# Output weights split in the first pass of the gated stage; eight scalings issued one at a time; last row tiles in order 0, 2, 1, 3

## Chip, cores and metric

The kernel runs on one core of a Trainium2 chip. The metric is the device time of one execution in microseconds (us). TensorE is called PE (its weight loads PEld), VectorE DVE, ScalarE ACT, GpSimd POOL; SP is SyncE, whose queue issues every DMA of this kernel.

## What is computed

Local-window and global attention over 4 batches give x of 2304 tokens by 512. Two feed-forward stages follow:

```
h = x @ w_in                      # 512 -> 2048
x = elu(h) @ w_out                # 2048 -> 512
rms = sqrt(mean(x*x, -1) + 1e-6)
xn = x / rms * rms_g
out = (silu(xn @ w_gate) * (xn @ w_val)) @ w_o2     # 512 -> 1536 -> 512
```

All is float32. The products run in PE's fp32r format: every operand is divided into a high part (an ACT cast) and the rest (a DVE subtraction), and three products of the parts (`PASSES`) are summed. Such a division is called a split below.

## The kernel before

**First stage.** `moe_block(b, slot)` works on 512 tokens, b from 0 to 3, in 16 slots j. A slot runs a first product `mm1` (12 matmuls into `h`), and a second product `mm2` of the slot before (12 matmuls into `y`); the attention of the next block lies between. Block 3 carries, in slots 0 to 9, the global attention (`g_S`, `g_T`, `g_PV`, `g_X`), and in slots 10 to 15 the 128 global rows' own first stage (`second_mm1`, `second_mm2`) and the preparation of the gated stage (`second_slot`: norms of y, splits of the operands).

**Output weights.** The gated stage multiplies 2x2 blocks by a Strassen-like scheme of seven products. The seven sums of blocks of `w_o2` are made in blocks 1 to 2 and written to DRAM as `wF`: 21 units of 128 x 512 floats (256 KB), two to a group, 11 groups. Before the change block 3 turns them into split form: in the last part of slots 0 to 8 and in the first two parts of slot 9, `h_split(n)` casts each unit of a group into a tile of the pool `stg` (two buffers), subtracts in place, and stores both parts to `wH` (42 stores of 256 KB); then `h_load` fetches the group after next into a pool of two buffers (`hp`). The gated stage reads `wH` back (`w_load`) when it needs it.

**Start of the gated stage.** At the end of slot 9 `second_start()` closes the pools of the global attention and issues the loads of the matrix of ones, of the first 1024 tokens of y (`ya`, `yb`, 1 MB each) and of the first three groups of input weights (`fetch`, 512 KB each into one of three `wraw` buffers). `y_square` (four ACT squares and three POOL sums), `y_root` (one PE product `ms`, a square root and a DVE reciprocal) and `y_norm` (four DVE scalings of 128 x 512) follow for each half.

**Gated stage.** `for k in range(2)` takes 1024 tokens at a time: six iterations i of 14 products (`product`, six matmuls of 512 columns each) with ACT copies (`take`), DVE sums (`add_to`), `gate` and `times`, into `p`; then seven passes n that multiply `p` by `wH`. The input weights come in 42 groups, 21 for each k: `need(q)` splits groups (an ACT cast and a DVE subtraction of 128 x 1024) one or two ahead of the product that uses them, and each split fetches a further group. Tiles of these splits, of `p` and of the operands `xc` share the 16 slots of the pool `wpool`. While k = 0 runs, the second 1024 tokens are prepared: `y_square(1, .)` at the ends of i = 1 and 2, `y_root(1, .)` within i = 2 and 3, `y_norm(1, 0)` and `y_norm(1, 1)` at the ends of i = 2 and 3, `y_sums(1)` at the end of i = 4.

**Last pass.** With k = 1 and n = 6, four row tiles t of 128 tokens are finished one after the other. `ch[0]` holds t = 0, 1 and `ch[1]` holds t = 2, 3. After each, half a bank is copied to an `o4` tile of `stg` and stored. The rows of the global tokens (`og`) leave through `stg` just before.

**Order.** PE runs its instructions in the order in which they are written. For the other engines and the DMA queue the framework orders the instructions at build time by a planner with its own cost estimates; `behind(mark)` tells it to place what is inside after the last pair of instructions noted in `mark`. Each engine then runs its list in order, so that an instruction which waits holds all behind it, and SP holds all DMAs behind one that waits.

Of the kernel before, what the change touches and what calls it, by code (L numbers as in the profile page):

```python
# [7 lines left out]
F32 = mybir.dt.float32  # L8
F32R = mybir.dt.float32r
# [4 lines left out]
ALU = mybir.AluOpType  # L14
# [19 lines left out]
def f(ap):  # L34
    return ap.bitcast(F32)
# [7 lines left out]
def fused_kernel(ctx: ExitStack, tc: tile.TileContext, kq, vl, gkq, gv, w_in, w_out, w_gate, w_val, w_o2, rms_g, consts, out):  # L43
# [102 lines left out]
    @contextmanager  # L146
    def behind(pair):
        with tc.issue_after(pair[0].ins), tc.issue_after(pair[1].ins):
            yield
# [447 lines left out]
        fetch()  # L597

    wraws, n_fetch, groups = [], [0], {}
    n_split, wmark = [0], []  # L600

    def fetch():
        while len(wraws) < 3 and n_fetch[0] < 42:
            raw = bpools["raw"].tile([P, 1024], F32, tag="wraw", name="wraw")
            parts, q, end = raw.rearrange("p (s a n) -> p s a n", s=4, a=2), 4 * (n_fetch[0] % 21), 4 * (n_fetch[0] % 21) + 4
            while q < end:
                i, r = divmod(q, 14)
                m = min(14 - r, end - q)
                nc.sync.dma_start(out=parts[:, 4 - (end - q):4 - (end - q) + m],
                                  in_=wS[i // 2, :, r:r + m, :, P * (i % 2):P * (i % 2) + P])  # L610
                q += m
            wraws.append(raw)
            n_fetch[0] += 1

    def split(n=1):
        for _ in range(n):
            if n_split[0] >= 42:
                return
            raw = wraws.pop(0).rearrange("p (a n) -> p a n", a=8)
            t = wpool.tile([P, 8, 2, P], F32R, tag="w", name="wS")  # L620
            groups[n_split[0]] = t
            n_split[0] += 1
            hi = nc.scalar.copy(t[:, :, 0, :], raw)  # L623
            wmark[:] = hi, nc.vector.tensor_tensor(out=t[:, :, 1, :], in0=raw, in1=f(t[:, :, 0, :]), op=ALU.subtract)  # L624
            fetch()

    def need(q):
        while q not in groups:
            with behind(mark):
                split()  # L630
# [30 lines left out]
            nc.vector.reciprocal(rs, rs)  # L661
            rs_[k, h] = rs

    def y_norm(k, h):
        if k < 2:
            y = ys_[k][h]
            for c in range(4):
                nc.vector.scalar_tensor_tensor(out=y[:, c], in0=y[:, c], scalar=gcol[:, c:c + 1], in1=rs_[k, h], op0=ALU.mult, op1=ALU.mult)

    def y_sums(k):  # L670
        if k < 2:
# [105 lines left out]
    def product(ps, k, i, pos, m, first=True):  # L777
        q, base = 14 * i + 2 * pos + m, 21 * k
        need(base + min(20, q // 4 + (q % 4 > 0) + 1))
        w, x = groups[base + q // 4], X[XSETS[pos]]  # L780
        for c in range(2):
            for z, (ws, xs) in enumerate(PASSES):
                nc.tensor.matmul(ps, w[:, 2 * (q % 4) + c, ws, :], x[:, c, xs, :], start=(first and c == 0 and z == 0), stop=(c == 1 and z == 2),  # L783
                                 skip_group_check=True)
# [86 lines left out]
    xd = xgp.tile([P, 2, 2, P], F32R, name="xd")  # L871
    with ExitStack() as gs:
        gp = gs.enter_context(tc.tile_pool(name="gp", bufs=1))
        hp = gs.enter_context(tc.tile_pool(name="hp", bufs=2))
        zero = gp.tile([P, 64], F32, name="zero")[:, 0:1]
        nc.vector.memset(zero, 0.0)
        G = {}
# [71 lines left out]
            nc.tensor.transpose(x[:64, :], d["e"], ident)  # L949
            nc.scalar.copy(xg32[64 * par:64 * par + 64, :, b * 32:b * 32 + 32], x[:64, :].rearrange("d (a q) -> d a q", a=4))  # L950

        wf_t = []

        def h_load():
            n = len(wf_t)
            if n < 11:
                t = hp.tile([P, 2, 2, 256], F32, tag="wf", name="wf")
                nc.sync.dma_start(out=t if n < 10 else t[:, :1], in_=wF[n] if n < 10 else wF[n, :, :1])
                wf_t.append(t)

        def h_split(n):
            for q in range(2 if n < 10 else 1):
                t = wf_t[n][:, q]
                hi = stg.tile([P, 2, 256], F32, tag="stg", name="wh")
                nc.scalar.copy(hi.bitcast(F32R), t)
                nc.vector.tensor_tensor(out=t.bitcast(F32R), in0=t, in1=hi, op=ALU.subtract)
                for z, part in enumerate((hi, t)):
                    nc.sync.dma_start(out=wH[n, :, q, z], in_=part)
            h_load()

        def slot3(j, part, h):
            g = act1(h, 512) if part == 0 else None
            b = j // 2
            if j < 8:
                if j % 2 == 0:
                    if part < 2:
                        g_S(b, part)
                    elif b:
                        g_PV(2 * b - 1)
                        g_load_v(2 * b + 1)  # L980
                        g_X(2 * b - 2)
                elif part < 2:
                    g_T(2 * b + part)
                else:
                    g_load_k(b + 1)
                    g_PV(2 * b)
                    g_load_v(2 * b + 2)
                    if b:
                        g_X(2 * b - 1)
            elif j == 8 and part == 2:  # L990
                g_PV(7)
                g_X(6)
            elif j == 9 and part == 0:
                g_X(7)
                xg32 = G["x"]
                nc.scalar.copy(xg[:, :, 0, :], xg32[:, :, :P])
                nc.vector.tensor_tensor(out=xg[:, :, 1, :], in0=xg32[:, :, :P], in1=f(xg[:, :, 0, :]), op=ALU.subtract)
            if j < 9 and part == 2 or j == 9 and part < 2:
                with behind(mark):
                    h_split(j + part * (j == 9))  # L1000
            if j == 9 and part == 2:
                gs.close()
                second_start()
            if j >= 10:
                if part == 0:
                    if 0 <= j - 11 < 4:
                        gg[j - 11] = g_act(gg.pop("e"))
                    if j - 12 < 3:
                        second_mm2(j - 12)
                    second_mm1(j - 10)  # L1010
                if part == 2:
                    second_slot(j - 10)
            return g
# [1 line left out]
        g_load_k(0)  # L1015
        g_load_v(0)
        g_load_v(1)
        h_load()
        h_load()
        moe_block(3, slot3)  # L1020
        second_mm2(3)
        ysb = moe.tile([P, 2, 512], F32, tag="xT3", name="ysb")
# [8 lines left out]
    for k in range(2):  # L1031
        pp = []
        for i in range(6):
# [15 lines left out]
            for z in range(2):  # L1049
                product(Q[z], k, i, 1, z)  # L1050
                add_to(t1[:, z], Q[z])
                if z == 0:
                    gate(t1[:, 0])
            times(p[:, 0], t1[:, 0], t1[:, 1])
            if k:
                if i == 0:
                    with behind(mark):
                        x_split(1, ("B22",))
                tile_products(i, 1)
            for z in range(2):  # L1060
                product(A[z], k, i, 2, z, False)
                take(t2[:, z], A[z])
                if z == 0:
                    if k == 0 and i == 1:
                        g_root(*yg)
                    elif i in (2, 3):
                        y_root(k + 1, i - 2)
            Q = [aps.tile([P, 512], F32, tag="att", name="Q") for _ in range(2)]
            for z in range(2):
                product(Q[z], k, i, 3, z)  # L1070
# [2 lines left out]
            for z in range(2):  # L1073
# [3 lines left out]
                if z == 0:  # L1077
                    gate(t3[:, 0])
            times(p[:, 3], t3[:, 0], t3[:, 1])
            for z in range(2):  # L1080
                product(A[z], k, i, 5, z, False)
            if k:
# [1 line left out]
            e = moe.tile([P, 512], F32, tag="e", name="s", bufs=2)  # L1084
            mark[0] = nc.scalar.activation(e, A[0], AF.Silu)
            times(p[:, 1], e, A[1])
            if i == 5:
                h_n, h_p, w_t = [0], [], []
                w_load(w_t)
                w_load(w_t)  # L1090
                for _ in range(3):
                    prepare(h_n, h_p, pp, k)
# [5 lines left out]
            times(p[:, 2], t2[:, 0], t2[:, 1])  # L1098
            nc.vector.tensor_tensor(out=p[:, 2], in0=p[:, 2], in1=p[:, 3], op=ALU.add)
            if k == 0:  # L1100
                if i == 0:
                    y_load(1)
                elif i == 1:
                    y_square(1, 0)
                elif i == 2:
                    y_square(1, 1)
                    y_norm(1, 0)
                elif i == 3:
                    y_norm(1, 1)
                elif i == 4:  # L1110
                    y_sums(1)

# [8 lines left out]
        for n in range(7):  # L1121
# [8 lines left out]
                    prepare(h_n, h_p, pp, k)  # L1130
            order_ = [(i, t) for i in range(6) for t in range(4)]
            if k and n == 6:
                order_ = [(i, t) for t in range(4) for i in range(6)]
            for i, t in order_:
                q = 6 * n + i
                while len(w_t) < min(11, q // 4 + 3):
# [18 lines left out]
                    elif n == 5:  # L1155
                        tile_out(i, 1, 1, w, False, i == 5)
                if k and n == 6 and i == 5:
                    if t % 2 == 0:
                        o4 = stg.tile([P, 512], F32, tag="stg", name="osb")
                    half = slice(256 * (t % 2), 256 * (t % 2) + 256)  # L1160
                    (nc.scalar.copy if t % 2 == 0 else nc.vector.tensor_copy)(o4[:, half], ch[t // 2][:, half])  # L1161
                    nc.sync.dma_start(out=rows(1, 1)[:, t, 0:256], in_=o4[:, half])
            if n == 0:
                for z in range(2):
                    nc.scalar.copy(a1[:, z], c1[z])
# [134 lines left out]
```

## Time and profile before

| | us |
|---|---|
| median of 3 runs (898.19 to 901.67) | 900.2 |
| profiled execution | 897.91 |
| its span, first to last instruction | 896.1 |
| PE busy | 856.2 |
| DVE busy | 631.0 |
| ACT busy | 465.3 |

The span is the part of the profiled execution that the trace covers. An engine's busy time is the union of its instructions; PE's matmuls are pipelined, so a busy PE can still run slowly. Lines L12 are lines of the kernel before. All times of the trace count from the span's start.

### The profile page before, as it was taken

Reading aid. Unit: us, or ns where it says so; the run is one execution under the profiler, and the core shown is the slowest. Engines: PE = TensorE matmul, PEld = TensorE weight load, DVE = VectorE, ACT = ScalarE, POOL = GpSimd, SP = SyncE. Lnnn points to the kernel's source line nnn. Section 1 sums busy time; section 2 is a strip of 40 time slices with the busy share of each in tenths; the row PEclk is TensorE's granted clock in tenths of the full one; section 3 lists DMA queues with packets and bytes.
Section 4 is the critical chain, followed back from the end, with each engine's and each line's share of the span. In section 5 each row is a group of like instructions: output and inputs, shape, how many; then the busy total and the mean of one; then the engine's idle time right before and its main releaser. Section 6 shows DMA issues by size and latency. Waiting matters only on the chain.

```text
span 896.1 us, 16399 instructions
## 1 busy us (share of the span) xinstructions
PE 856.2 (96%) x6706; PEld 711.7 (79%) x6706; DVE 631.0 (70%) x1094; ACT 465.3 (52%) x800; POOL 16.9 (2%) x16
## 2 busy tenths in 40 slices
PE   4789999999999999998979999999999999999998
PEld 3567777888888888766758887778999888888997
DVE  4899988767687686654459768886877665555673
ACT  4677665555565444543354567644555444443442
POOL 0000000000000000000030002100000000000000
PEclk9999999999999999999979999999999999999999
DMA  9785375766677766888840353337613323229102
GB/s 358 301 305 197 117 264 198 257 227 214 214 279 245 257 221 239 289 294 285 258 148 0 100 160 99 88 94 272 268 48 119 93 75 92 82 63 403 64 25 83
DMA packets 92592, 165.70 MB, mean 185 GB/s; under 512 B 5221, under 2 KB 59749, under 8 KB 87397
## 3 DMA queue, kind: packets, MB, share of 16 engines
q1 hardware_dynamic: 92516, 164.65, 53.2%
q8 instruction: 53, 0.87, 0.4%
q14 instruction: 23, 0.18, 0.1%
HBM read 128.45 MB, written 36.18 MB: 184 GB/s over the span
## 4 chain that ended last, share of the span: by engine, by line
PE 74%; DVE 10%; DMA 7%; ACT 4%; issue 2%; SPq 1%; POOL 0%; ACTq 0%; DVEq 0%
PE y L154 15%; PE h L133 15%; PE c L1146 13%; PE A L783 12%; PE Q L783 10%; DMA wH<-wf 2%; PE pg L797 2%; DMA kq<-in_kq 2%; DVE dx L93 1%; PE yg L715 1%; PE s L244 1%; DVE dx L94 1%; DMA wf<-wF 1%; PE ptp L272 1%; PE o L285 1%
## 5 line engine op out<-in xcount | busy, mean ns | idle before, releaser
L154 PE MATMUL y<-g,wA 128*128 128x512 f32 x768 | 197.8, 401 | 4.7 <-DVE g L141 4.0
L133 PE MATMUL h<-xT,wA 128*128 128x512 f32 x768 | 188.6, 395 | 1.3 <-DVE xT L310 1.3
L154 PEld LDWEIGHTS y<-g,wA 128*128 128x128 f32 x768 | 140.2, 189 | 40.4 <-DVE g L141 5.7
L133 PEld LDWEIGHTS h<-xT,wA 128*128 128x128 f32 x768 | 144.5, 189 | 33.3 <-DVE xT L310 2.1
L783 PE MATMUL A<-xc,wS 128*128 128x512 f32 x576 | 138.8, 392 | 0.4 <-DVE pp L836 0.4
L1146 PE MATMUL c<-wH,p 128*128 128x256 f32 x1008 | 125.8, 283 | 1.1 <-ACT osb L1161 1.1
L783 PEld LDWEIGHTS A<-xc,wS 128*128 128x128 f32 x576 | 107.0, 188 | 23.7 <-issue 1.0
L1146 PEld LDWEIGHTS c<-wH,p 128*128 128x128 f32 x1008 | 123.1, 192 | 1.7 <-ACT osb L1161 1.5
L783 PE MATMUL Q<-xc,wS 128*128 128x512 f32 x432 | 104.8, 391 | 0.8 <-DVE t L827 0.7
L783 PEld LDWEIGHTS Q<-xc,wS 128*128 128x128 f32 x432 | 80.0, 188 | 18.5 <-DVE t L827 2.0
L827 DVE TENSOR_TENSOR t<-t,Q 128x512 f32<-128x512 f32 x72 | 48.8, 685 | 56.0 <-ACT t L830 36.5
L822 ACT CAST p<-pp 128x512 fp32r<-128x512 f32 x84 | 51.4, 620 | 55.6 <-PE c L1146 52.3
L830 ACT COPY t<-A 128x512 f32<-128x512 f32 x72 | 42.2, 586 | 65.8 <-PE A L783 65.7
L823 DVE TENSOR_TENSOR p<-pp,p 128x512 fp32r<-128x512 f32 x84 | 57.0, 688 | 24.2 <-ACT p L822 23.8
L624 DVE TENSOR_TENSOR wS<-wraw,wS 128x1024 fp32r<-128x1024 f32 x42 | 52.3, 1246 | 21.7 <-ACT wS L623 21.5
L122 ACT ACTIVATE e<-h 128x512 f32<-128x512 f32 x48 | 28.9, 602 | 73.8 <-PE h L133 73.8
L140 ACT CAST g<-e 128x512 fp32r<-128x512 f32 x64 | 39.7, 620 | 49.1 <-DVE e L124 35.2
L141 DVE TENSOR_TENSOR g<-e,g 128x512 fp32r<-128x512 f32 x64 | 44.4, 694 | 12.5 <-ACT g L140 12.0
L124 DVE SCALAR_TENSOR_TENSOR e<-e,h 128x512 f32<-128x512 f32 x48 | 32.5, 677 | 28.9 <-ACT e L123 28.9
L623 ACT CAST wS<-wraw 128x1024 fp32r<-128x1024 f32 x42 | 43.9, 1045 | 7.0 <-DMA wraw<-wS 7.0
L84 ACT ACTIVATE dx<-raw 128x1024 f32<-128x1024 f32 x34 | 39.0, 1150 | 10.9 <-DMA raw<-in_moe_w_out 4.3
L833 ACT ACTIVATE t<-t 128x512 f32<-128x512 f32 x36 | 22.8, 633 | 40.4 <-DVE t L827 40.4
(202 smaller groups left out, 972.7 us busy)
## 6 DMA issues: line engine op xcount, KB each, us to landing
wH<-wH SPq DMA_DIRECT2D x20, 1024.0 KB, 6.9
wraw<-wS SPq DMA_DIRECT2D x36, 512.0 KB, 3.8
raw<-in_moe_w_out SPq DMA_DIRECT2D x14, 1024.0 KB, 6.6
raw<-in_moe_w_in SPq DMA_DIRECT2D x8, 1024.0 KB, 7.0
raw<-in_moe_w_gate SPq DMA_DIRECT2D x6, 1024.0 KB, 5.6
raw<-in_moe_w_val SPq DMA_DIRECT2D x6, 1024.0 KB, 6.0
wS<-raw SPq DMA_DIRECT2D x24, 256.0 KB, 2.3
wH<-wh SPq DMA_DIRECT2D x21, 256.0 KB, 5.5
```

What stands on the lines that cost most here:

```text
L133: nc.tensor.matmul(h[:, :n], W1[c, G][:, ws, o:o + P], xT[c][:, xs, :n], start=(k == 0), stop=(k == 11))
L140: hi = nc.scalar.copy(g[:, 0, :n], e[:, :n])
L141: mark[:] = hi, nc.vector.tensor_tensor(out=g[:, 1, :n], in0=e[:, :n], in1=f(g[:, 0, :n]), op=ALU.subtract)
L154: nc.tensor.matmul(ys[dc][:, :n], W2[j][:, ws, dc * P:(dc + 1) * P], g[:, gs, :n], start=(j == 0 and k == 0), stop=(j == 15 and k == 2))
L623: hi = nc.scalar.copy(t[:, :, 0, :], raw)
L624: wmark[:] = hi, nc.vector.tensor_tensor(out=t[:, :, 1, :], in0=raw, in1=f(t[:, :, 0, :]), op=ALU.subtract)
L783: nc.tensor.matmul(ps, w[:, 2 * (q % 4) + c, ws, :], x[:, c, xs, :], start=(first and c == 0 and z == 0), stop=(c == 1 and z == 2), skip_g ...
L822: hi = nc.scalar.copy(p[:, 0, :], src)
L823: mark[:] = hi, nc.vector.tensor_tensor(out=p[:, 1, :], in0=src, in1=f(p[:, 0, :]), op=ALU.subtract)
L827: mark[1] = nc.vector.tensor_tensor(out=t, in0=t, in1=ps, op=ALU.add)
L830: mark[0] = nc.scalar.copy(t, ps)
L1146: nc.tensor.matmul(ch[t // 2][:, 256 * (t % 2):256 * (t % 2) + 256], p[:, pl, t * P:(t + 1) * P], w[:, wl, :], start=(n in (0, 1, 3) and i ...
```

## The change

Three edits:

- `hp`, `h_load` and `h_split` go. The 11 groups of `wF` become items of the list that `fetch` and `split` work through: one behind each of the input-weight groups 2, 3, 4, 6, 7, 8, 10, 13, 14, 16 and 17, so all within the first five iterations of k = 0. Such an item (a "piece") is loaded into a `wraw` buffer (512 KB), cast and subtracted at full width (128 x 1024, the last one 128 x 512) into a `wpool` tile, and stored to `wH` by one DMA of 1 MB. `product` splits a waiting piece at every fourth product.
- The eight scalings of `y_norm(1, .)` are issued one at a time (`norm_next`) at four places of an iteration, from the middle of i = 2 to the start of i = 4.
- The last pass takes its row tiles in the order 0, 2, 1, 3, its two `o4` tiles are both asked for ahead, and ACT copies tiles 0 and 1, DVE 2 and 3.

```diff
+    pieces = {g: n for n, g in enumerate((2, 3, 4, 6, 7, 8, 10, 13, 14, 16, 17))}
+    items = []
+    for g in range(42):
+        items += [(0, g)] + ([(1, pieces[g])] if g in pieces else [])
...
-        while len(wraws) < 3 and n_fetch[0] < 42:
+        while len(wraws) < 3 and n_fetch[0] < len(items):
+            kind, g = items[n_fetch[0]]
...
+            if kind:
+                m = 2 if g < 10 else 1
+                nc.sync.dma_start(out=raw.rearrange("p (q a n) -> p q a n", q=2, a=2)[:, :m], in_=wF[g, :, :m])
...
+    def split():
...
+        if kind:
+            m = 2 if g < 10 else 1
+            raw = raw.rearrange("p (q a n) -> p q a n", q=2, a=2)[:, :m]
+            t = wpool.tile([P, 2, 2, 2, 256], F32R, tag="w", name="wG")[:, :m]
+            hi, lo = t[:, :, 0], t[:, :, 1]
...
+        nc.scalar.copy(hi, raw)
+        nc.vector.tensor_tensor(out=lo, in0=raw, in1=f(hi), op=ALU.subtract)
+        if kind:
+            nc.sync.dma_start(out=wH[g, :, :m], in_=f(t))
+        fetch()
...
+    to_norm = []
+
+    def norm_next():
+        if to_norm:
+            h, c = to_norm.pop(0)
+            with behind(mark):
+                y_norm(1, h, (c,))
...
+        if q % 4 == 3 and wraws and wraws[0][0]:
+            with behind(mark):
+                split()
...
-        hp = gs.enter_context(tc.tile_pool(name="hp", bufs=2))
...
-        def h_split(n):
-            for q in range(2 if n < 10 else 1):
-                t = wf_t[n][:, q]
-                hi = stg.tile([P, 2, 256], F32, tag="stg", name="wh")
-                nc.scalar.copy(hi.bitcast(F32R), t)
-                nc.vector.tensor_tensor(out=t.bitcast(F32R), in0=t, in1=hi, op=ALU.subtract)
-                for z, part in enumerate((hi, t)):
-                    nc.sync.dma_start(out=wH[n, :, q, z], in_=part)
-            h_load()
...
-            if j < 9 and part == 2 or j == 9 and part < 2:
-                with behind(mark):
-                    h_split(j + part * (j == 9))
...
-                    elif i in (2, 3):
-                        y_root(k + 1, i - 2)
+                    elif k == 0 and i in (2, 3):
+                        y_root(1, i - 2)
+                        to_norm += [(i - 2, c) for c in range(4)]
...
-                    y_norm(1, 0)
-                elif i == 3:
-                    y_norm(1, 1)
...
-                order_ = [(i, t) for t in range(4) for i in range(6)]
+                order_ = [(i, t) for t in (0, 2, 1, 3) for i in range(6)]
+                o4 = [stg.tile([P, 512], F32, tag="stg", name="osb") for _ in range(2)]
...
-                    (nc.scalar.copy if t % 2 == 0 else nc.vector.tensor_copy)(o4[:, half], ch[t // 2][:, half])
-                    nc.sync.dma_start(out=rows(1, 1)[:, t, 0:256], in_=o4[:, half])
+                    o, half = o4[t // 2], slice(256 * (t % 2), 256 * (t % 2) + 256)
+                    (nc.scalar.copy if t < 2 else nc.vector.tensor_copy)(o[:, half], ch[t // 2][:, half])
+                    nc.sync.dma_start(out=rows(1, 1)[:, t, 0:256], in_=o[:, half])
```

## Rows read from the trace of the kernel before

**Rows 1.** The page, part 1: busy us, share of the span, instructions.

```profile
PE 856.2 (96%) x6706; PEld 711.7 (79%) x6706; DVE 631.0 (70%) x1094; ACT 465.3 (52%) x800; POOL 16.9 (2%) x16
```

**Rows 2.** Windows, slots 2 to 7 of block 3: us, busy by engine, PEclk, DMA share, GB/s.

```profile
370.45:378.70 8.25, 8.25 (x105) 5.34 (x98) 4.69 (x15) 2.92 (x6) 0.00 (x0) 1.00 1.05 379
378.70:386.36 7.66, 7.66 (x79) 6.09 (x77) 3.85 (x13) 3.94 (x10) 0.00 (x0) 1.00 1.00 373
386.36:395.08 8.72, 8.72 (x100) 5.44 (x99) 4.97 (x17) 3.52 (x8) 0.00 (x0) 1.00 0.81 275
395.08:404.39 9.31, 7.91 (x79) 6.03 (x77) 4.23 (x12) 4.04 (x9) 0.00 (x0) 1.00 0.75 248
404.39:414.46 10.07, 8.32 (x101) 5.32 (x99) 4.71 (x15) 2.71 (x5) 0.00 (x0) 1.00 0.96 299
414.46:423.74 9.28, 7.88 (x80) 6.01 (x77) 4.88 (x14) 5.45 (x12) 0.00 (x0) 1.00 0.81 267
```

**Rows 3.** Waits of ACT, 380 to 464 us: total us, times, longest.

```profile
ACT wh L965 <- DMA wf<-wF: 9.4, 4, 4.3
...
ACT wh L965 <- issue: 7.5, 2, 4.6
```

**Rows 4.** Timeline of PE, slots 11 and 12: start, us, what; in brackets idle before.

```profile
444.28 2.88 PE L133 MATMUL h<-xT,wA 128*128 128x512 f32 x12
450.97 1.11 PE L706 MATMUL egt<-ident,e 128*128 128x128 f32 x4 [3.81 <-DVE e L116]
451.73 5.22 PE L699 MATMUL hg<-wA,xg 128*128 128x512 f32 x12
...
462.63 1.41 PE L658 MATMUL ms<-acc,ones 128*128 128x512 f32 x2 [2.94 <-POOL acc L652]
463.19 4.93 PE L133 MATMUL h<-xT,wA 128*128 128x512 f32 x12
```

**Rows 5.** Timeline of SP, where slot 9 ends and slot 10 runs.

```profile
436.69 0.59 SPq L639 DMA_DIRECT2D yb<-yT  x1
440.99 0.33 SPq L958 DMA_DIRECT2D wf<-wF  x1
...
444.80 1.96 SPq L639 DMA_DIRECT2D ya<-yT  x1
```

**Rows 6.** Timeline of ACT, slots 10 and 11.

```profile
446.95 1.04 ACT L623 CAST wS<-wraw 128x1024 fp32r<-128x1024 f32 x1 [6.95 <-DMA wraw<-wS]
...
454.92 1.15 ACT L651 ACTIVATE sq<-ya 128x512 f32<-128x512 f32 x2 [5.92 <-DMA ya<-yT]
```

**Rows 7.** Windows, iterations i = 0 to 4 of k = 0; columns as in rows 2.

```profile
508.80:528.00 19.20, 19.20 (x88) 15.88 (x86) 11.85 (x15) 10.98 (x17) 0.00 (x0) 1.00 0.74 226
528.00:547.50 19.50, 19.50 (x88) 15.80 (x86) 14.23 (x22) 14.53 (x22) 1.02 (x1) 1.00 0.35 101
547.50:569.50 22.00, 20.90 (x86) 15.98 (x87) 19.84 (x22) 14.61 (x21) 7.58 (x6) 1.00 0.25 72
569.50:589.80 20.30, 20.29 (x88) 16.09 (x87) 17.57 (x22) 12.72 (x17) 0.00 (x0) 1.00 0.37 105
589.80:609.20 19.40, 19.34 (x85) 15.66 (x84) 14.62 (x18) 8.66 (x14) 0.00 (x0) 1.00 0.31 88
```

**Rows 8.** Groups of DVE instructions in these five iterations: busy us, mean ns.

```profile
L624 DVE TENSOR_TENSOR wS<-wraw,wS 128x1024 fp32r<-128x1024 f32 x17 | 21.8, 1282 | 2.0 <-ACT wS L623 1.8
```

**Rows 9.** DMA issues in i = 0: KB each, median us to landing.

```profile
wraw<-wS SPq DMA_DIRECT2D x3, 512.0 KB, 5.8
...
yb<-yT SPq DMA_DIRECT2D x1, 1024.0 KB, 5.3
```

**Rows 10.** The chain that ended last, end of the kernel: start, us, what.

```profile
884.09 5.99 DMA out<-osb
```

**Rows 11.** Timeline of PE, last pass.

```profile
885.35 4.58 PE L1146 MATMUL c<-wH,p 128*128 128x256 f32 x36 [0.46 <-ACT osb L1161]
890.61 2.41 PE L1146 MATMUL c<-wH,p 128*128 128x256 f32 x18 [0.68 <-ACT osb L1161]
```

More of the change, by code (lines that the diff above doesn't have):

```diff
@@ L599, in fused_kernel @@
     wraws, n_fetch, groups = [], [0], {}
-    n_split, wmark = [0], []
+    pieces = {g: n for n, g in enumerate((2, 3, 4, 6, 7, 8, 10, 13, 14, 16, 17))}
+    items = []
+    for g in range(42):
+        items += [(0, g)] + ([(1, pieces[g])] if g in pieces else [])
     def fetch():
-        while len(wraws) < 3 and n_fetch[0] < 42:
+        while len(wraws) < 3 and n_fetch[0] < len(items):
+            kind, g = items[n_fetch[0]]
             raw = bpools["raw"].tile([P, 1024], F32, tag="wraw", name="wraw")
[L605 to L612, printed above, removed]
-            n_fetch[0] += 1
@@ L615, in split @@
[L615 to L625, printed above, removed]
+            if kind:
+                m = 2 if g < 10 else 1
+                nc.sync.dma_start(out=raw.rearrange("p (q a n) -> p q a n", q=2, a=2)[:, :m], in_=wF[g, :, :m])
+            else:
+                parts, q, end = raw.rearrange("p (s a n) -> p s a n", s=4, a=2), 4 * (g % 21), 4 * (g % 21) + 4
+                while q < end:
+                    i, r = divmod(q, 14)
+                    m = min(14 - r, end - q)
+                    nc.sync.dma_start(out=parts[:, 4 - (end - q):4 - (end - q) + m],
+                                      in_=wS[i // 2, :, r:r + m, :, P * (i % 2):P * (i % 2) + P])
+                    q += m
@@ new lines, in fetch @@
+            wraws.append((kind, g, raw))
+            n_fetch[0] += 1
+    def split():
+        if not wraws:
+            return
+        kind, g, raw = wraws.pop(0)
+        if kind:
[3 more added lines that the diff above has]
+            hi, lo = t[:, :, 0], t[:, :, 1]
+        else:
+            raw = raw.rearrange("p (a n) -> p a n", a=8)
+            t = groups[g] = wpool.tile([P, 8, 2, P], F32R, tag="w", name="wS")
+            hi, lo = t[:, :, 0, :], t[:, :, 1, :]
+        nc.scalar.copy(hi, raw)
[3 more added lines that the diff above has]
+        fetch()
@@ L662, in y_root, with y_norm @@
             rs_[k, h] = rs
[L664 to L668, printed above, removed]
+    def y_norm(k, h, cs=range(4)):
+        y = ys_[k][h]
+        for c in cs:
+            nc.vector.scalar_tensor_tensor(out=y[:, c], in0=y[:, c], scalar=gcol[:, c:c + 1], in1=rs_[k, h], op0=ALU.mult, op1=ALU.mult)
+    to_norm = []
[4 more added lines that the diff above has]
+                y_norm(1, h, (c,))
     def y_sums(k):
@@ L950, in g_X @@
             nc.scalar.copy(xg32[64 * par:64 * par + 64, :, b * 32:b * 32 + 32], x[:64, :].rearrange("d (a q) -> d a q", a=4))
[L952 to L959, printed above, removed]
-        def h_split(n):
-            for q in range(2 if n < 10 else 1):
-                t = wf_t[n][:, q]
-                hi = stg.tile([P, 2, 256], F32, tag="stg", name="wh")
-                nc.scalar.copy(hi.bitcast(F32R), t)
-                nc.vector.tensor_tensor(out=t.bitcast(F32R), in0=t, in1=hi, op=ALU.subtract)
-                for z, part in enumerate((hi, t)):
-                    nc.sync.dma_start(out=wH[n, :, q, z], in_=part)
-            h_load()
         def slot3(j, part, h):
@@ L1017, in fused_kernel @@
         g_load_v(1)
-        h_load()
-        h_load()
         moe_block(3, slot3)
@@ L1054, in fused_kernel @@
             times(p[:, 0], t1[:, 0], t1[:, 1])
+            norm_next()
             if k:
@@ L1079, in fused_kernel @@
             times(p[:, 3], t3[:, 0], t3[:, 1])
+            norm_next()
             for z in range(2):
@@ L1086, in fused_kernel @@
             times(p[:, 1], e, A[1])
+            norm_next()
             if i == 5:
@@ L1100, in fused_kernel @@
             if k == 0:
+                norm_next()
                 if i == 0:
@@ L1157, in fused_kernel @@
                 if k and n == 6 and i == 5:
-                    if t % 2 == 0:
-                        o4 = stg.tile([P, 512], F32, tag="stg", name="osb")
-                    half = slice(256 * (t % 2), 256 * (t % 2) + 256)
-                    (nc.scalar.copy if t % 2 == 0 else nc.vector.tensor_copy)(o4[:, half], ch[t // 2][:, half])
-                    nc.sync.dma_start(out=rows(1, 1)[:, t, 0:256], in_=o4[:, half])
+                    o, half = o4[t // 2], slice(256 * (t % 2), 256 * (t % 2) + 256)
+                    (nc.scalar.copy if t < 2 else nc.vector.tensor_copy)(o[:, half], ch[t // 2][:, half])
+                    nc.sync.dma_start(out=rows(1, 1)[:, t, 0:256], in_=o[:, half])
             if n == 0:
```

## The prediction

> **What bounds the kernel.** The page's busy line comes first: PE is busy 96% of the span, DVE 70%, ACT 52% [rows 1]. So time can only be won where PE idles or runs at its lower clock, and the question is where that is. Cut by stages, the windows show it in block 3, from slot 4 on, and in a smaller measure in iteration i = 2 of the gated stage's first pass (22.0 us where its neighbours take 19.5 and 20.3) [rows 2, 7].
>
> In block 3 even slots have one content and odd slots another (the global attention alternates). Slots 2 and 3 take 8.25 and 7.66 us with PE busy throughout. Slots 4 and 6, with slot 2's content, take 8.72 and 10.07; slots 5 and 7, with slot 3's, take 9.31 and 9.28 [rows 2]. The excess is 0.47 + 1.65 + 1.82 + 1.62 = 5.56 us. The waits name a cause: ACT stood still before the cast of `h_split` for 9.4 us for a load of `wF`, and for 7.5 us more in two waits that the profile puts on nothing else [rows 3]. ACT runs in order, so the copies that PE needs for the global attention stand behind that cast.
>
> Slots 11 and 12 lose more. PE idles 3.81 us before `egt` and 2.94 us before `ms`. After each, matmuls that take 2.88 us for twelve at 2.4 GHz take 5.22 and 4.93: the lower level of the clock, for 2.34 + 2.05 us [rows 4]. Together 11.1 us. Both waits go back to SP: the load of `yb` was issued at 436.69, the next thing in the queue is the last `wF` load at 440.99, and only then come `wraw` and, at 444.80, `ya` [rows 5]. ACT held still 6.95 us for `wraw`, with the exponential that `egt` needs behind it, and 5.92 us for `ya`, with the norm that `ms` needs [rows 6]. The four views tell one story: PE waits for ACT, ACT for DMA, SP for `h_split`.
>
> **What leaving block 3 is worth.** Everything above that can come back is 5.56 + 11.1 = 16.7 us; with `h_split` gone, its 21 casts, 21 subtractions, 11 loads and 42 stores all leave the block.
>
> The first part I take whole: nothing else of slots 4 to 7 waits on a DMA for long. The second I do not. `ya` still has to be loaded, squared, summed and brought to `ms`. Without the last `wF` load, SP reaches `ya` 440.99 - (436.69 + 0.59) = 3.7 us sooner, and the block runs 5.56 us earlier: issue at 435.5. Landing takes between 5.3 us (a 1 MB load in a quieter place [rows 9]) and the 454.92 - 444.80 = 10.1 us of now, and from there to `ms` it took 462.63 - 454.92 = 7.7 us. So `ms` is ready between 448.5 and 453.3. PE would come to it at 462.63 - 5.56 - (3.81 + 2.34 + 2.94) = 448.0. A wait of 0.5 to 5.3 us stays; a shorter chain through ACT could make it 0. I take 2.0, nearer to the short landing since the block's 42 stores, 10.7 MB in all, no longer share the DMA engines, and 0.7 for some matmuls at the lower clock behind it. Worth of this edit: **16.7 - 2.7 = 14.0 us**, bounds 9 and 16.7.
>
> **What the pieces cost in the gated stage.** A piece is one ACT cast and one DVE subtraction of the size of an input-weight group, 1.28 us on DVE [rows 8]; ten and a half of them are 13.4 us. Group g is split when product 4(g - 2) + 1 comes up, and a piece two products later, so 3 pieces fall into i = 0, 3 into i = 1, then 1, 2 and 2. DVE is the engine to watch, for ACT is at 75% at most (14.53 of 19.5 us in i = 1) [rows 7].
>
> Nothing shows how full DVE may get before PE waits, but i = 2 is the nearest row: DVE 19.84 of 22.0 us, 90%, and PE behind. I let every iteration be as long as its DVE work over 0.90, if that is longer than now. The scalings move too: one of four (0.64 us, half of a 128 x 1024 subtraction) leaves i = 2 for i = 3, one leaves i = 3 for i = 4, and one of the three subtractions of `y_sums`, which now runs in i = 3, comes behind the last scaling in i = 4 (1.28). Then:
>
> i = 0: (11.85 + 3.84) / 0.9 = 17.4, below 19.2, so 0. i = 1: (14.23 + 3.84) / 0.9 = 20.1, +0.6. i = 2: (19.84 - 0.64 + 1.28) / 0.9 = 22.8, +0.8. i = 3: (17.57 + 2.56 - 1.28) / 0.9 = 20.9, +0.6. i = 4: (14.62 + 0.64 + 1.28 + 2.56) / 0.9 = 21.2, +1.8. Sum **3.8 us**. The bounds are 0, if idle time takes them all (the five iterations have 100.4 - 78.1 = 22.3 us of it on DVE), and 13.4, if every subtraction lies on PE's path.
>
> The scalings one by one give a little inside this: four in a row behind a reciprocal no longer hold the sums that release PE's banks. I keep that in the 0.90, as no row separates it.
>
> **DMA.** Six pieces in i = 0 and 1 move 6 x 1.57 = 9.4 MB. At the 379 GB/s of a full window [rows 2] that is 24.9 us of transfer, beside 0.74 x 19.2 + 0.35 x 19.5 = 21.0 us there already [rows 7]: 45.9 us of work in 38.7. The DMA engines end i = 1 up to 7.2 us late. Stores are late for nobody at once: PE reads `wH` after i = 5. Loads matter: three `wraw` buffers mean that an item is fetched some six products (6 x 19.2 / 14 = 8.2 us) before ACT reaches it, less the split of 2 to 3 us ahead of the fetch; landing is 5.8 us now [rows 9]. That cover is just used up. If it breaks, ACT stands still before the cast, as it did in slots 4 to 7 under the same load, where it cost 5.56 us. Bounds 0 and 5.6; I take **1.2**, low because slots 2 and 3, with the DMA share at 1.0, lost nothing.
>
> The trace's 379 GB/s stand against a lower figure of the Trainium skill (DMA: Bandwidth & Descriptors, Specifications), which puts HBM at about 358 GB/s for a core. By it the 15.8 MB of both iterations, the earlier traffic included, would take 44 us, an estimate: 5.3 us late, where the rows give 7.2. Either leaves the term and its bounds as they stand.
>
> **Last row tiles.** Now tile 1 waits 0.46 us and tile 3 0.68 us for the copy out of the bank they share with the tile before [rows 11]. In the order 0, 2, 1, 3 the first goes: tile 2 starts 0.46 earlier, at 884.89, and with 2.29 us a tile ends at 887.2. Its copy needs a second `stg` buffer, and that is the one from which `og` is stored until 884.09 + 5.99 = 890.08 [rows 10]. Tile 3 is in tile 2's bank, so it waits for this copy: 890.1 + 0.4 = 890.5, against 890.61 now. The wait for the bank becomes a wait for the buffer: **0**, bounds 0 and -1.1.
>
> **Sum.** -14.0 + 3.8 + 1.2 + 0 = -9.0 us on the profiled 897.9 (a span of 896.1 with 1.8 around it): 888.9. That execution lies 2.3 below the median of the runs, so the forecast for the median is **891**.
>
> **Rivals.** (a) All comes back and idle time hides the pieces: -16.7, 883.5 as median. For it: DVE idles 22 us; against it, the chain to `ms`. (b) The stall at `ms` and `egt` stays whole, because `ya` lands as late as now: -5.6 + 5.0 = -0.6, 899.6. For it: the order on SP is the planner's; against: the `wF` load that held `ya` is gone. (c) Every DVE microsecond of the pieces is on the path: -14.0 + 13.4 + 1.2 = +0.6, 900.8. For it: i = 2. (d) The other side: `wraw` comes late in i = 0 and 1, and ACT stands still before each of six pieces as before the first group now, 6.95 us [rows 6]. Less a cover of two products, 2.7, that is 4.2 x 6 = 25 us: -14.0 + 3.8 + 25 = +15, 915. It turns the sign from (14.0 - 3.8) / 6 = 1.7 us a piece.
>
> **Chances.** Forecast 0.60 (its own range 886 to 896), (a) 0.12, (b) 0.12, (c) 0.10, (d) 0.06. A measurement of this kernel can tell 0.5%, 4.5 us, from no change: below 895.7 is faster. The forecast nearly always, (a) always, (b) and (c) three times in ten give that: 0.77. Same 0.17: most of (b) and (c). Slower 0.06: (d). The range reaches from (a) to (b): 883 to 899.
>
> **What would show it.** Block 3: slots 4 to 7 at 8.25 and 7.66 us, no idle PE before `egt`, some before `ms`. Gated stage: i = 1 to 4 at 20 to 23 us with DVE at about 90%; the casts of pieces with idle time before them, "DMA wraw", if the loads are late. End: tile 3 waiting for the copy of tile 2. The forecast fails if PE still waits some 7 us in slots 11 and 12, or if the five iterations grow by more than 9.

## The result, and the profile after

The changed kernel takes 886.5 us (median of 4 runs, 885.1 to 887.0) against 899.2 for the kernel before on the same chips; the ratio is 0.9855 with a 95% interval of 0.9825 to 0.9885. The forecast was 891, with 883 to 899 as its range. The profiled execution fell from 897.9 to 887.0 us, its span from 896.1 to 884.4.

Cut at the same places, the two spans differ by -11.7 us: block 3 starts 0.8 us later (356.6 against 355.8, ahead of anything the change touches), lasts 135.5 us in place of 152.6 (-17.1); the products of the gated stage's first pass last 123.8 in place of 119.5 (+4.4); all the rest is 268.1 in place of 267.9 (+0.2).

Block 3 first. The windows of slots 4 to 7 after the change answer to the last four lines of [rows 2]:

```profile
387.15:395.38 8.23, 8.23 (x102) 5.32 (x99) 3.64 (x14) 2.03 (x4) 0.00 (x0) 1.00 0.41 117
395.38:403.06 7.68, 7.68 (x79) 6.08 (x77) 3.00 (x10) 3.36 (x9) 0.00 (x0) 1.00 0.48 201
403.06:411.28 8.22, 8.22 (x101) 5.31 (x99) 3.64 (x14) 2.02 (x4) 0.00 (x0) 1.00 0.27 82
411.28:418.96 7.68, 7.68 (x79) 6.08 (x77) 3.00 (x10) 3.36 (x9) 0.00 (x0) 1.00 0.27 87
```

Each slot is as long as PE is busy, and as long as slots 2 and 3 were. The DMA share has gone from 0.75 to 0.96 down to 0.27 to 0.48. PE's timeline of slots 11 and 12, beside [rows 4]:

```profile
442.10 0.60 PE L728 MATMUL egt<-ident,e 128*128 128x128 f32 x4
442.45 3.02 PE L721 MATMUL hg<-wA,xg 128*128 128x512 f32 x12
...
448.03 1.02 PE L673 MATMUL ms<-acc,ones 128*128 128x512 f32 x2
448.49 3.34 PE L133 MATMUL h<-xT,wA 128*128 128x512 f32 x12
```

No idle time is left, and no group of twelve takes 5 us: the clock stays at its upper level. What SP did there, beside [rows 5]:

```profile
429.07 0.59 SPq L654 DMA_DIRECT2D yb<-yT  x1
429.71 4.72 SPq L617 DMA_DIRECT2D wraw<-wS  x3
434.47 1.68 SPq L654 DMA_DIRECT2D ya<-yT  x1
```

The gap of 3.7 us behind `yb` is gone. ACT's timeline, beside [rows 6], shows what came of it:

```profile
436.27 1.05 ACT L636 CAST wS<-wraw 128x1024 fp32r<-128x1024 f32 x1 [1.54 <-DMA wraw<-wS]
...
441.70 0.63 ACT L661 ACTIVATE acc<-ya 128x512 f32<-128x512 f32 x1 [3.37 <-DMA ya<-yT]
```

ACT still waits for `ya`, but 3.37 us, and it starts on it 7.2 us after the issue (10.1 before). What follows is shorter too. POOL's timeline after the change, and then the line of ACT's timeline before it that answers to 441.70:

```profile
442.93 4.11 POOL L667 TENSOR_TENSOR acc<-acc,sq 128x512 f32<-128x512 f32 x3 [442.49 <-DMA wraw<-wF]
```

```profile
457.44 0.64 ACT L646 ACTIVATE acc<-ya 128x512 f32<-128x512 f32 x1
```

Before, POOL's sums started from a square (`acc`) that ACT made only at 457.44, 2.5 us after it had begun on `ya`, as other work stood ahead of it, a cast of `h_split` among it. Now this square is made first, and the sums are ready at 442.93 + 4.11 = 447.04, 5.3 us after ACT began on `ya` (7.7 before). PE reaches `ms` at 448.03, a microsecond after it is ready.

Now the gated stage. The windows of i = 0 to 4, beside [rows 7]:

```profile
492.49:512.47 19.98, 19.70 (x88) 15.62 (x86) 13.01 (x16) 11.46 (x17) 0.00 (x0) 1.00 0.84 270
512.47:535.16 22.69, 20.62 (x87) 15.53 (x86) 18.71 (x27) 16.86 (x24) 0.00 (x0) 1.00 0.94 314
535.16:557.01 21.85, 20.20 (x87) 16.01 (x86) 20.74 (x18) 18.09 (x26) 10.63 (x6) 1.00 0.82 264
557.01:578.24 21.23, 20.24 (x87) 16.07 (x86) 19.00 (x23) 14.41 (x19) 0.00 (x0) 1.00 0.65 205
578.24:597.28 19.04, 19.04 (x85) 15.77 (x84) 18.12 (x24) 9.99 (x15) 0.00 (x0) 1.00 0.82 253
```

The loss lies mainly in i = 0 and 1 (+0.8, +3.2); i = 3 adds 0.9, and i = 2 and 4 are 0.15 and 0.4 shorter. In i = 0 and 1 DVE is busy 65% and 82%, and the DMA share is 0.84 and 0.94. In i = 4, with DVE at 95%, nothing is lost: 19.04 us, less than the 19.40 of before. The waits of ACT in this stretch:

```profile
ACT wS L636 <- DMA wraw<-wS: 10.2, 7, 4.8
```

The longest of the seven, in ACT's timeline at the start of i = 1:

```profile
514.12 1.05 ACT L636 CAST wS<-wraw 128x1024 fp32r<-128x1024 f32 x1 [4.77 <-DMA wraw<-wS]
515.35 1.05 ACT L636 CAST wG<-wraw 128x1024 fp32r<-128x1024 f32 x1 [0.18 <-DMA wraw<-wF]
516.30 0.63 ACT L858 ACTIVATE t<-t 128x512 f32<-128x512 f32 x1
```

Here `gate`, at 516.30, stood behind two casts, the first of which had waited for its load. PE's timeline has the same wait one step on; it stops until the subtraction behind that cast is done:

```profile
516.48 2.56 PE L808 MATMUL Q<-xc,wS 128*128 128x512 f32 x10 [0.53 <-DVE wS L637]
```

The DMA issues of i = 0, beside [rows 9], say why:

```profile
wraw<-wS SPq DMA_DIRECT2D x2, 512.0 KB, 9.8
```

A group of input weights lands 9.8 us after its issue; it was 5.8.

The last pass: its chain and PE's timeline answer to [rows 10, 11].

```profile
872.17 5.99 DMA out<-osb
...
878.29 0.44 DVE osb L1162
```

```profile
870.63 6.65 PE L1149 MATMUL c<-wH,p 128*128 128x256 f32 x54
878.76 2.42 PE L1149 MATMUL c<-wH,p 128*128 128x256 f32 x18 [1.49 <-DVE osb L1162]
```

Three tiles now run without a break, and the fourth waits 1.49 us, for the copy that waits for the store of `og`. Before, two waits made 1.14.

### The profile page after: what moved, and what is told of

Same layout as the page of the kernel before. It is cut to its first block, busy times and chain, and to the rows that moved or that the text cites. A ratio compares the mean times of both kernels' runs of the same rounds, so it can differ in the third digit from the quotient of the medians.

```text
span 884.4 us, 16312 instructions
## 1 busy us (share of the span) xinstructions
PE 853.3 (96%) x6706; PEld 710.2 (80%) x6706; DVE 629.1 (71%) x1084; ACT 463.1 (52%) x790; POOL 18.7 (2%) x16
## 4 chain that ended last, share of the span: by engine, by line
PE 76%; DVE 9%; DMA 7%; ACT 4%; issue 2%; POOL 1%; SPq 0%; DVEq 0%; ACTq 0%
PE y L154 16%; PE h L133 16%; PE c L1149 13%; PE A L808 11%; PE Q L808 8%; DMA raw<-in_moe_w_in 2%; PE pg L822 2%; DMA wraw<-wS 2%; PE o L285 2%; PE ptp L272 1%; PE s L244 1%; DVE dx L93 1%; DVE dx L94 1%; PE hg L721 1%; PE yg L737 1%
## 5 line engine op out<-in xcount | busy, mean ns | idle before, releaser
L636 ACT CAST wS<-wraw 128x1024 fp32r<-128x1024 f32 x42 | 43.9, 1046 | 11.7 <-DMA wraw<-wS 11.7
L93 DVE SCALAR_TENSOR_TENSOR dx<-raw,dx 128x1024 int32<-128x1024 int32 x34 | 42.5, 1257 | 0.8
```

The lines of the kernel that those rows point to most:

```text
L93: nc.vector.scalar_tensor_tensor(out=i32(x), in0=word[:, :, 1], scalar=-0x40000000, in1=i32(x), op0=ALU.bitwise_and, op1=ALU.bitwise_or)
L636: nc.scalar.copy(hi, raw)
```

## Experiments

All times are medians; the kernel before, on the same chip, took 898.9 to 899.4 in these comparisons. "Block 3" in this section counts from the first product of the global attention (`gs`) to its end: 149.8 us before, 132.7 after. "Products" are the six iterations of k = 0 with the transpose ahead of them: 119.8 before, 124.2 after. Block 3 starts between 354.5 and 357.8 us in the profiled executions, with no edit of the output weights, the scalings or the last pass ahead of it; so differences of up to 3 us between two kernels are read from these stages here, and not from the whole time.

**e1: the two smaller edits alone.** `h_split` and `h_load` stay in block 3.

```diff
-    pieces = {g: n for n, g in enumerate((2, 3, 4, 6, 7, 8, 10, 13, 14, 16, 17))}
+    pieces = {g: n for n, g in enumerate((), 11)}
...
+                with behind(mark):
+                    h_split(j + part * (j == 9))
```

> The two smaller edits alone (scalings one by one, last row tiles in order 0, 2, 1, 3); the output weights are split in block 3 as before. Theory: both are worth nothing that can be measured, 898 to 900 us as the kernel before, block 3 152 to 153 us long, tile 3 of the last pass held by the copy of tile 2. Rival: the scalings in a row were what made i = 2 of the gated stage long (22.0 us), so that i = 2 falls by 2 us and the time to 897.

Measured: 897.0 us, 0.9981 (0.9967 to 0.9995). Block 3 is 151.6 us, with the same two stalls in PE's timeline:

```profile
451.86 1.11 PE L728 MATMUL egt<-ident,e 128*128 128x128 f32 x4 [3.54 <-DVE e L116]
...
464.34 2.07 PE L673 MATMUL ms<-acc,ones 128*128 128x512 f32 x2 [4.75 <-POOL acc L667]
```

The products take 118.3 us, 1.5 less than before. Its windows of i = 2 and 3:

```profile
549.56:570.82 21.26, 20.82 (x88) 16.10 (x87) 16.84 (x18) 14.60 (x22) 7.77 (x6) 1.00 0.26 75
570.82:590.76 19.94, 19.94 (x87) 16.15 (x86) 16.48 (x20) 12.51 (x17) 0.00 (x0) 1.00 0.37 106
```

21.3 and 19.9 where [rows 7] have 22.0 and 20.3. So the scalings are worth about 1.5 us by the trace, less than the rival's 2 in i = 2 alone, and more than nothing. (The time is the rival's 897, but i = 2 gave only 0.7 of it.) It also gives the pieces' own cost: 124.2 - 118.3 = 5.9 us.

**e2: eight groups stay in block 3, three become pieces.**

```diff
-    pieces = {g: n for n, g in enumerate((2, 3, 4, 6, 7, 8, 10, 13, 14, 16, 17))}
+    pieces = {g: n for n, g in enumerate((14, 16, 17), 8)}
...
+            if j < 8 and part == 2:
+                with behind(mark):
+                    h_split(j)
```

> Groups 0 to 7 of the output weights are split in slots 0 to 7 of block 3 as before, only groups 8, 9 and 10 become pieces (behind input groups 14, 16, 17). Theory (the queue): slots 11 and 12 lose their 11 us because the last wF load stands ahead of wraw and ya on SP; they come back, slots 4 to 7 still lose their 5.6, and the gated stage loses nothing: some 888 us. Rival (the traffic): the stores of eight groups alone keep the DMA engines so late that ya lands as late as before; then 899.

Measured: 885.7 us, 0.9849 (0.9826 to 0.9872), as good as the full change. Block 3 is 140.1 us, 7.4 more than after the change. Lines of PE's timeline in slots 5 to 7 and 11:

```profile
400.85 0.28 PE L949 MATMUL gpb<-ident,gpp 128*32 128x128 f32 x1 [1.43 <-ACT xg L975]
...
410.15 0.69 PE L930 MATMUL gs<-gkq 64*32 64x272 f32 x16 [1.84 <-ACT xg L975]
...
419.73 0.63 PE L948 MATMUL gpa<-ident,gpp 128*128 128x128 f32 x4 [1.27 <-DVE gst L940]
...
454.30 1.02 PE L673 MATMUL ms<-acc,ones 128*128 128x512 f32 x2
```

The waits of slots 5 to 7 are there as before, and those of slots 11 and 12 are gone: the two losses of block 3 have separate causes, and the second needs only the last three groups gone. With them go the last `wF` load, their stores and their casts, all at once; the run does not tell these apart. The products take 118.6 us, so three late pieces cost them nothing.

**e3 and e4: fewer pieces in i = 0 and 1.** e3 splits groups 0 to 3 in slots 0 to 3 and leaves seven pieces; e4 keeps eleven pieces and starts them later.

```diff
-    pieces = {g: n for n, g in enumerate((2, 3, 4, 6, 7, 8, 10, 13, 14, 16, 17))}
+    pieces = {g: n for n, g in enumerate((6, 8, 10, 13, 14, 16, 17), 4)}          # e3
+    pieces = {g: n for n, g in enumerate((4, 6, 8, 9, 10, 11, 12, 13, 14, 16, 17))}   # e4
```

> Groups 0 to 3 are split in slots 0 to 3 of block 3, where the trace of before shows no loss; groups 4 to 10 become pieces behind input groups 6, 8, 10, 13, 14, 16, 17, so none in i = 0, two in i = 1. Theory (late loads cost the gated stage its 4.4 us, in i = 0 and 1): block 3 stays at 135.5 us, the gated stage loses under 1.5, some 883.5 us. Rival (DVE full above 90%): i = 2, 3 and 4 lose 3 us as each has the same pieces as in the full change; 885.5 or more. Third: the backlog of slots 0 to 3 spills into slots 4 and 5 and costs 2 us, 886 to 887.

> All eleven groups are pieces, but behind input groups 4, 6, 8, 9, 10, 11, 12, 13, 14, 16, 17: one in i = 0, two in i = 1, three each in i = 2 and 3, two in i = 4. Theory (late loads in i = 0 and 1): the two lose 1 us in place of 4, i = 2 and 3 up to 1 more each; 883 to 885 us. Rival (DVE full): two more subtractions in i = 2, where DVE is at 95%, and one more in i = 3 lie on the path, +3.8 us there; 888 to 890.

Measured: e3 884.6 us, 0.9842 (0.9824 to 0.9860); e4 884.8 us, 0.9846 (0.9826 to 0.9865). Block 3 is 133.2 in e3: four groups in slots 0 to 3 cost 0.5. The windows of i = 0 to 2 in e3:

```profile
492.48:511.68 19.20, 19.20 (x87) 15.78 (x86) 11.85 (x15) 10.95 (x17) 0.00 (x0) 1.00 0.75 229
511.68:531.70 20.02, 19.66 (x88) 15.91 (x87) 15.08 (x22) 14.38 (x21) 0.00 (x0) 1.00 0.55 175
531.70:555.37 23.67, 21.78 (x88) 17.07 (x86) 19.56 (x21) 17.41 (x25) 9.41 (x6) 0.93 0.65 200
```

and of i = 2 in e4:

```profile
531.94:555.64 23.70, 20.77 (x87) 15.92 (x86) 21.62 (x22) 19.11 (x27) 8.86 (x6) 1.00 0.76 243
```

In both, i = 0 and 1 together take 39.2 us in place of 42.7, which speaks for late loads (fewer pieces lighten DVE too; e5 and e6 tell these apart). But i = 2 grows to 23.7, from 21.85, in e4 with more pieces there than in the full change, in e3 with no more. Each theory had missed that; e10 looks into it. In e3 most of the 1.8 us is the lower clock (0.93 in that window; the last section has the lines), in e4, with the clock at 1.00, PE idles 2.93 us in that window in place of 1.65.

**e5 and e6: one cost of a piece doubled.** e5 makes every subtraction twice, e6 every store.

```diff
+        if kind:                                                                  # e5
+            nc.vector.tensor_tensor(out=lo, in0=raw, in1=f(hi), op=ALU.subtract)
...
+            nc.sync.dma_start(out=wX[g, :, :m], in_=f(t))                         # e6
```

> The full change, with every subtraction of a piece made twice on DVE (the same values written again): 13 us more DVE work in i = 0 to 4, the same DMAs. Theory (the gated stage's loss comes from late loads, DVE has room): i = 0 and 1 within 1 us of the full change, the iterations with DVE at 95% (i = 2, 4) grow by 1 to 2 us each, together +2 to +4. Rival (the 0.90 rule of the prediction): every subtraction counts, 10.5 x 1.28 / 0.9 = +15 us.

> The full change, with every piece stored twice (once more to a second place in DRAM that nobody reads): 10.7 MB more DMA traffic in i = 0 to 4, the same work on ACT and DVE. Theory (late loads): 6 MB more in i = 0 and 1 are 16 us of transfer at 379 GB/s, i = 0 to 2 grow by 5 to 15 us. Rival (DVE): within 1 us of the full change.

Measured: e5 891.3 us, 0.9919 (0.9901 to 0.9938); e6 907.5 us, 1.0092 (1.0069 to 1.0116). The windows of i = 0 and 1 in e5:

```profile
491.53:512.16 20.63, 19.95 (x87) 15.54 (x86) 15.10 (x18) 11.75 (x18) 0.00 (x0) 1.00 0.85 281
512.16:533.50 21.34, 20.36 (x87) 15.68 (x86) 19.89 (x28) 17.53 (x25) 0.00 (x0) 1.00 0.85 289
```

and of i = 0 to 2 in e6:

```profile
493.19:513.26 20.07, 19.77 (x87) 15.63 (x86) 13.02 (x16) 11.90 (x18) 0.00 (x0) 1.00 0.84 284
513.26:542.05 28.79, 23.29 (x87) 17.52 (x86) 17.65 (x25) 18.04 (x27) 3.86 (x3) 0.88 0.83 311
542.05:570.61 28.56, 24.39 (x88) 17.74 (x86) 19.29 (x21) 16.44 (x22) 4.31 (x3) 0.88 0.91 315
```

With twice the subtractions i = 1 is 1.35 us shorter than in the full change; with twice the stores it is 6.1 longer, and i = 2 another 6.7. That settles i = 1: what counts there is the traffic of the DMAs, not DVE. It does not settle the 0.8 us of i = 0: that iteration takes 20.07 us with the stores doubled, hardly more than the 19.98 of the full change, and 0.65 more with the subtractions doubled. PE's one wait there, 0.28 us at 505.45 in the full change, is for an ACT copy that stands behind two casts of splits, one of them a piece's; which engine sets those 0.8 us is not shown.

The products of e5 are 5.1 us longer, so i = 2 and later grow by 5.8, 3.8 of it in i = 2, where PE waits 3.9 us before `ms` for POOL's sums. There more DVE work does count. 13 us more work cost 5.1, more than the theory's 2 to 4 and far from the rival's 15. In e6 the products are 20.5 us longer: i = 0 to 2 by 12.9, within the 5 to 15 forecast, and the iterations behind them by 7.6, which had not been forecast.

**e7: the last copies in another buffer.**

```diff
-                o4 = [stg.tile([P, 512], F32, tag="stg", name="osb") for _ in range(2)]
+                o4 = moe.tile([P, 4, 512], F32, tag="x32", name="osb")
+                o4 = [o4[:, 0], o4[:, 1]]
```

> The full change, but the two tiles that take the last pass's copies lie in the buffer of the first half of y, free by then, in place of the pool from which the global rows are being stored. Theory: the order 0, 2, 1, 3 gave nothing because tile 2's copy waits for that store; free of it the idle time before the last 18 matmuls (1.49 us) goes and the last DMA starts 1.4 to 1.5 us earlier: 885. Rival: the bank is the limit in another way, or the last store lands no earlier: no change.

Measured: 883.3 us, 0.9831 (0.9814 to 0.9848). PE's timeline of the last pass has all four tiles in one piece:

```profile
869.02 8.81 PE L1150 MATMUL c<-wH,p 128*128 128x256 f32 x72
```

From the end of the gated stage's first products to the end of the span it is 266.3 us in place of 268.1. The wait was for the buffer. The time lies 1.7 below the 885 forecast for another reason: of the 3.4 us that its span is shorter, only 1.8 lie in this stretch, 0.9 lie ahead of block 3 and 0.7 in the products.

**e8: the scalings in rows of four, with the pieces.**

```diff
-                        to_norm += [(i - 2, c) for c in range(4)]
...
+                    y_norm(1, 0)
+                elif i == 3:
+                    y_norm(1, 1)
```

> The full change with the scalings in rows of four, at the ends of i = 2 and 3, as before. Theory: with DVE at 95% in i = 2, a row of four scalings behind a reciprocal and a piece holds the sums that free PE's banks: i = 2 and 3 together 1 to 3 us longer, 888 to 889. Rival: the order of the scalings is worth nothing, within 0.5 us of the full change.

Measured: 889.2 us, 0.9905 (0.9881 to 0.9930); the products take 127.6 us, 3.4 more than in the full change. The window of i = 2:

```profile
533.24:558.30 25.06, 21.95 (x87) 16.77 (x86) 23.45 (x24) 18.76 (x27) 10.42 (x6) 0.93 0.81 264
```

25.1 us in place of 21.85. With pieces beside them the spread scalings are worth more than alone in e1. In part this is the clock: PE waits 2.45 us before `ms` (1.65 in the full change), and `ms` and the six matmuls behind it then take 2.04 + 3.03 us in place of 1.10 + 1.94.

**e9: put together.** Four groups in slots 0 to 3, the other pieces away from i = 2, the buffer of e7.

```diff
+    pieces = {g: n for n, g in enumerate((4, 6, 7, 12, 13, 16, 17), 4)}
```

> Put together from what the runs before showed: groups 0 to 3 split in slots 0 to 3 of block 3; the other seven as pieces behind input groups 4, 6, 7, 12, 13, 16, 17, so that none falls into the stretch of i = 2 in which POOL sums squares; the last pass's copies in the buffer of the first half of y. Theory: block 3 stays at 133 us from the first product of the global attention, the five iterations fall from 104.8 to some 100.5, the last pass gives 1.5: 880 to 881.5 us. Rival (the idle time before ms in i = 2 comes from the iteration's own DVE work, whatever pieces there are): i = 2 stays at 22 to 23.7 and the time at 883.

Measured: 882.8 us, 0.9822 (0.9805 to 0.9839), the lowest of the kernels that compute everything, but not told apart from e7. Block 3 is 132.8 and the last pass runs through. The five iterations take 102.9 us, better than 104.8 but not 100.5: i = 2 takes 21.9 and i = 3 22.1, so the rival (i = 2 at 22 or more, 883) came nearer than the theory (880 to 881.5). PE's timeline there:

```profile
541.09 1.10 PE L673 MATMUL ms<-acc,ones 128*128 128x512 f32 x2 [1.27 <-DVE t L852]
...
567.17 1.67 PE L808 MATMUL Q<-xc,wS 128*128 128x512 f32 x6 [1.19 <-ACT rs L675]
```

**e10: POOL's sums left out.**

```diff
-                nc.gpsimd.tensor_tensor(out=acc, in0=acc, in1=sq, op=ALU.add)
+                if k == 0:
+                    nc.gpsimd.tensor_tensor(out=acc, in0=acc, in1=sq, op=ALU.add)
```

> The full change with the three POOL sums of squares of the second 1024 tokens left out (only the first square goes into the norm of these tokens, so their values change). Theory: in i = 2 subtractions that read two tiles of on-chip memory run at 2.3 us beside POOL in place of 1.2, and hold the sum that ms waits behind; without POOL the 1.65 us before ms go and i = 2 falls from 21.85 to 20 to 20.5 us, the time by some 2 us. Rival (DVE is simply full, or loads are late): i = 2 falls by under 0.7 us.

Measured: 883.3 us, 0.9826 (0.9810 to 0.9842). The wait before `ms` went, but i = 2 is 22.1 us. Its window, and then a line of the timeline:

```profile
532.23:554.36 22.13, 20.54 (x88) 15.91 (x86) 17.55 (x19) 17.94 (x26) 0.00 (x0) 1.00 0.90 293
```

```profile
543.97 0.69 ACT L676 ACTIVATE rs<-ms,cst 128x512 f32<-128x512 f32 x1
...
544.71 1.65 PE L809 MATMUL Q<-xc,wS 128*128 128x512 f32 x6 [1.59 <-ACT rs L676]
```

The theory fell, although the time is 3.2 us below the full change's: of these, 2.1 lie ahead of block 3 and 1.0 in the products, none of it in i = 2. PE waited 1.59 us five microseconds later instead. `ms` sits in one of the two banks that `Q` uses, and ACT takes its square root only after what stands ahead of it. So i = 2 has two waits, one behind DVE's sums beside POOL and one behind ACT's list, and without the first the second takes its time.

**e11: eight groups in block 3, four of them not stored.** The lines are set against e2; the gated stage reads groups 0 to 3 in place of 4 to 7.

```diff
-                for z, part in enumerate((hi, t)):
+                for z, part in enumerate((hi, t) if n < 4 else ()):
```

> As the run with eight groups in block 3, but groups 4 to 7 are not stored (the loads, casts and subtractions stay; the gated stage reads groups 0 to 3 in their place, so the values of the output change). Theory: slots 4 to 7 lose their 5.6 us because casts wait for buffers whose stores have not landed, and for loads held behind these stores; without them block 3 from the first product of the global attention is 133 us long and not 140, the time 879 to 880. Rival (the work of the split on ACT and DVE, in front of the copies that PE needs): 139 to 140 us, 885.

Measured: 882.6 us, 0.9815 (0.9795 to 0.9836); this kernel writes 4 MB less and is no candidate. Block 3 is 134.4 us, against e2's 140.1. PE keeps a single wait of over a microsecond in slots 4 to 7, in slot 5, where the stores of groups 0 to 3 may not have landed:

```profile
401.20 0.29 PE L949 MATMUL gpb<-ident,gpp 128*32 128x128 f32 x1 [1.33 <-ACT xg L975]
```

The time lies above the 879 to 880 forecast: block 3 is 1.4 us longer than the 133 that was expected, and starts 2.0 us later than in e2. The rival's 139 us are far off. The casts, subtractions and loads alone cost little; what held slots 4 to 7 was in the main the stores.

## Why the prediction was right, and where not

**Block 3, slots 4 to 7.** Forecast 5.56 us back; they came back whole. The cause as told, ACT behind casts that wait for DMAs, holds in e2 and e11, with the stores as its root.

**Block 3, slots 11 and 12.** Forecast 11.1 less 2.7 that stay; nothing stayed. This term was mis-sized: `ya` was issued at 434.47 (435.5 forecast) and PE came to `ms` at 448.03 (448.0 forecast), but `ya` was in use 7.2 us after its issue, and the chain behind it took 5.3 us, where 7.7 had been carried over from a stretch in which a cast of `h_split` stood ahead of the first square. So `ms` was ready at 447.04, before the 448.5 to 453.3 forecast. The cause as told, the last `wF` load ahead of `ya` on SP, is shown in part. Its 3.7 us on SP are as long as PE's wait before `egt` (3.81); before `ms` the shorter landing (2.9 us) and the shorter chain (2.4 us) came on top. e2, with eight groups of stores still there, has the stalls gone, but it takes away that load together with the stores and casts of the last three groups; what each was worth is not shown. Together block 3 gave 17.1 where 14.0 were forecast.

**Gated stage.** The net +4.4 lies close to the forecast +5.0, but for other reasons; that the two agree is luck. Step "every iteration as long as its DVE work over 0.90" failed: i = 4 ran at 95% without a loss, and in e5 i = 1 was no longer with DVE at 93% (19.89 of 21.34 us) than at 82%. The DMA term, taken at 1.2 within bounds of 0 and 5.6, is the one that was mis-sized: i = 1 alone lost 3.2, which e5 and e6 put down to it (the 0.8 of i = 0 they do not): the cover of some 8 us for a load was said to be just used up at 5.8 us of landing, and landing rose to 9.8. Slots 2 and 3, which lost nothing at a DMA share of 1.0, were the wrong row to lean on; slots 4 to 7 were the right one. The 7.2 us of lateness rest on a DMA share and a rate together; from bytes alone, 15.8 MB at the same 379 GB/s take 41.7 us, 3.0 us late, so the sum was rougher than it looked. e6 shows the mechanism of rival (d), with the stores doubled: up to 600 us of its trace ACT waits 7.8 us for loads of input weights and PE 11.7 us for splits, and the kernel is slower than before.

**Scalings.** Left inside the 0.90 as something no row separates; they gave 1.5 us alone (e1) and 3.4 beside the pieces (e8). Without them the pieces would have cost the products 127.6 - 119.8 = 7.8 us.

**Last row tiles.** Forecast 0, for the buffer of `og`; the trace and e7 bear out both the wait and its cause.

**Sum.** -9.0 forecast, -11.7 in the span. Block 3 gave 3.1 more than forecast and the products cost 0.6 less, less 0.2 in the rest and the 0.8 by which block 3 started later. The rivals (b) and (c) did not come: `ya` landed early, and DVE had room. Rival (a) was right about block 3 and wrong about the pieces, which idle time did not hide.

What stays open is the cost in i = 2 and 3. It moves between a wait for DVE's sums and a wait for ACT's square root as pieces are moved (e3, e4, e9, e10), and no run removed both. In e3, e5 and e8 the lower clock behind `ms` adds to it.

## What to carry to other kernels

When work waits on an in-order queue, look for what the waiting instruction holds up two queues further: here a load on SP that waited for a store kept others back for 3.7 us, and with the late landing and the longer ACT list behind it PE lost 11 us. e2 shows that moving three groups of eleven away was enough for that part. Work moved to a place with idle engines is paid in the resource that is nearest its limit there; set each one's load before and after the move against the time, the DMA engines too, and lean on the row in which that resource already cost something. A reordering that removes one wait should be followed to the next owner of the buffer: the new tile order only paid once its copies had a buffer of their own.

## What the runs showed of the hardware

In i = 2 of e3 PE stood idle for 1.89 us before `ms`, and the six matmuls behind it took 3.53 us, where they take 1.94 in the full change; the granted clock of that window is 0.93. From 540.5 to 545.0 us it is 0.62, so that for most of this time PE ran at the lower of its two levels (1.2 and 2.4 GHz). The length of that idle time alone does not decide: 1.65 us at the same place in the full change left the clock at 1.00, and so did 1.90 us in e4, where the six matmuls took 1.94. What does decide is not shown. The line of e4's timeline, then those of e3's:

```profile
540.79 1.10 PE L673 MATMUL ms<-acc,ones 128*128 128x512 f32 x2 [1.90 <-DVE t L852]
```

```profile
536.36 2.31 DVE L637 TENSOR_TENSOR wG<-wraw,wG 128x1024 fp32r<-128x1024 f32 x1
...
538.59 1.21 DVE L637 TENSOR_TENSOR wS<-wraw,wS 128x1024 fp32r<-128x1024 f32 x1
...
540.55 1.51 PE L673 MATMUL ms<-acc,ones 128*128 128x512 f32 x2 [1.89 <-DVE t L852]
...
541.08 3.53 PE L808 MATMUL A<-xc,wS 128*128 128x512 f32 x6
```

The first two lines of e3 show the same subtraction at 2.31 us beside POOL's sums (532.9 to 537.6 in this run) and at 1.21 after them. In e10, without POOL, the one at this place took 1.23. The Trainium skill has the rule for it (SBUF — State Buffer, Who interferes with whom): a DVE instruction with two inputs in SBUF contends with a GpSimd instruction that reads SBUF. The trace agrees.
